# Linear attention into a gated mixture of four causal heads: identity and mask from GpSimd's selections, with another written-out order

## The chip, the cores and the metric

One core of a Trainium2 chip runs the whole computation. The metric is the device time of one execution in microseconds (us); the number to compare is the median of several executions. The engines are named as the profile names them: PE is TensorE (matmuls; PEld are its weight loads), DVE is VectorE, ACT is ScalarE, POOL is GpSimd, and SP only issues DMAs.

## The reference

Inputs are `q`, `k`, `v` of 8 batches x 8 heads x 576 positions x 64, a feature matrix `w_phi` of 64x128, a gate, and projections for four experts. All is float32.

```python
def phi(x):
    proj = np.einsum('bhsd,df->bhsf', x, w_phi)
    proj = proj - np.max(np.abs(proj), axis=-1, keepdims=True)
    return np.concatenate([np.exp(proj), np.exp(-proj)], axis=-1)
q_p, k_p = phi(q), phi(k)
kv = np.einsum('bhsf,bhsd->bhfd', k_p, v)
z = np.sum(k_p, axis=2)
num = np.einsum('bhsf,bhfd->bhsd', q_p, kv)
den = np.einsum('bhsf,bhf->bhs', q_p, z)[..., None] + 1e-06
x = (num / den)            # heads side by side: 8 x 576 x 512
...
logits = x @ w_gate        # four experts, the best two are kept
for e in range(4):
    q, k, v = x @ wq[e], x @ wk[e], x @ wv[e]
    scores = 0.125 * (q @ k.transpose(0, 2, 1))
    scores = np.where(causal, -1000000000.0, scores)
    scores = scores - scores.max(-1, keepdims=True)
    a = np.exp(scores)
    a /= a.sum(-1, keepdims=True) + 1e-09
    out += gate_e * (a @ v @ wo[e])
```

## The kernel before, in words

The first half (linear attention) goes over 32 pairs of heads, four pairs to a batch. For a pair, PE projects the keys (`stream_k`, `stream_tail`), DVE takes the largest absolute value of each row and subtracts it (`center`, L413 and L415), ACT makes the two exponentials (`ek`), and PE sums them against `v` (`stream_kv`). The queries are projected with features on the partitions (`stream_q`), ACT or DVE copies them out (`evac_u`), POOL finds the largest absolute value across the partitions (`reduce`, L535), DVE subtracts it (L545), ACT makes two exponentials, and PE multiplies with `kv` (`stream_n`). DVE and ACT divide (`normed`), DVE transposes 32x32 blocks, and the rows go through HBM and come back as `xb`, split into a high and a low part for PE (a cast on ACT or DVE, then a subtraction on DVE, L183). For the first five pairs the queries are taken in plain float32 (L514), later ones split (L518).

The second half (`stream_b`) goes over 8 batches and two groups of two experts. It projects queries, keys, values and the gate (L178), makes the scores (L678), adds the causal mask on DVE (`soft`, L706), finds the maximum on POOL (`first_top`'s selections at L693, then `tops` at L535), subtracts on DVE (L813), exponentiates on ACT, multiplies with the values (L427), normalises, and projects out (L178). The identity is read only at the end, where the last batch's result is transposed on PE (`turned`, L473). The mask is read from the first scores on.

All these streams are Python generators. `Plan.loop` takes their steps in the order of a table of characters, `PICKS`: of each two characters the first names the stream that takes its next step, the second the PSUM bank, or whether ACT or DVE does a copy that either could do. `in_order` then fixes that order on each engine, so every engine runs its own list strictly one after the other. The table also sets the order in which SP issues DMAs. One thing more is fixed by hand: DVE instructions with SBUF operands are noted in `plan.port`, and each of POOL's maxima waits for the one noted last (`plan.behind`), so that the two don't run at the same time.

`constants` (L225 to L236) makes the identity and the mask on DVE by fifteen small instructions: a row of column numbers by doubling, a transposed column of row numbers, and comparisons. It is called where the first batch's second half begins to be planned (L749), with two not yet used pieces of the scores' buffer as scratch.

Of the kernel before, what the change touches and what calls it, by code (L numbers as in the profile page):

```python
# [11 lines left out]
AF = mybir.ActivationFunctionType  # L12
# [45 lines left out]
    "DISASASASIF-UAUAVAVAOAUAQACAPAQATARATAOAJEPAFAFAKaJAKAJARADAPAMALAF-FIxANADAOAHAyAxAQAKsKANARAJHJAAAEBOAPAPAPAHARABAvAGA"
    "FAIAwAFAGAQAvATAUGQAQATHQASCLABAGAAALAtAOArAoAtAqAsAoAoAoAsAqApAOAMAnAVDqApAoAmAFsFIYaFIFAD-oAqApAqAoApAYIoArArAFsYaYIrA"
    "qApApAFstApApApItAqAqAqApAlADAlANADAD-SEoAnAqAlAnATFPDSCRAiAiAlAlABAAALAKAKAOGOBjAlAcAgANHEAjAKALAiAKAcAjACACAhAcAgAfAFA"  # L60
    "cAIaIAjAhAiADAcADAHFHAdIMAcAHAcAiAiAiAiIiALALAaAAAaAcAgAfAKALAfAfAFAbAHCeAaAfAcAEGIsIAHAEDgAeAgALABAeACALAYAKAKAaAZAZAfA"
# [941 lines left out]
```

## Time and profile before

| what | us |
|---|---|
| median of 3 runs | 531.89 (531.48 to 532.16) |
| the profiled execution's own time | 530.78 |
| its span | 529.0 |
| PE busy | 521.7 (99%) |
| DVE busy | 489.7 (93%) |
| ACT busy | 383.6 (73%) |
| POOL busy | 205.5 (39%) |

The span runs from the first to the last instruction of the profiled execution; the 1.78 us by which its own time is longer lie outside it. Busy times are unions over an engine's instructions, without the instructions that only wait or issue DMAs. A matmul's end is modelled, so a full PE is not PE at its peak. "Idle before <- X" tells whose instruction ended an engine's idle time. The granted clock of PE is at its higher level of 2.4 GHz all through (0.999 on average).

### The profile page before, as it was taken

The numbers are of one execution on the slowest core, as the hardware profiler recorded it, in microseconds if no ns is written. First come the engines' busy times: TensorE is split into PE (matmuls) and PEld (weight loads), VectorE is DVE, ScalarE is ACT, GpSimd is POOL, SyncE is SP. The second block draws the span as 40 slices with busy tenths as digits, with TensorE's granted clock in tenths as the row PEclk, the third lists the DMA queues.
The fourth block names the chain that finished last, engine by engine and source line by source line (L and its number), as shares of the span: only waits on it lengthen the run. The fifth ranks groups of instructions, "written<-read, shape, count | busy, mean of one in ns | idle before, by whom it ended". The sixth has DMA issues, their size and how long they took to land.

```text
span 529.0 us, 21993 instructions
## 1 busy us (share of the span) xinstructions
PE 521.7 (99%) x9422; PEld 503.8 (95%) x9422; DVE 489.7 (93%) x1020; ACT 383.6 (73%) x713; POOL 205.5 (39%) x112
## 2 busy tenths in 40 slices
PE   8999999999999999999999999999999999999997
PEld 6999999999999999999999999999999999999996
DVE  5999999999999999999999999989997999997984
ACT  4999879798697976975866687686686656565562
POOL 4755373063352457206270326332564060212430
PEclk9999999999999999999999999999999999999999
DMA  8888466534842546654455544476463324523213
GB/s 206 222 207 209 126 173 169 127 95 124 195 115 76 137 113 190 164 167 123 108 138 150 148 140 121 131 188 176 101 171 115 101 53 128 156 80 101 69 70 113
DMA packets 102674, 72.69 MB, mean 137 GB/s; under 512 B 57136, under 2 KB 84144, under 8 KB 102576
## 3 DMA queue, kind: packets, MB, share of 16 engines
q1 hardware_dynamic: 102272, 70.93, 50.5%
q8 instruction: 74, 1.21, 1.0%
q10 hardware_dynamic: 304, 0.34, 0.2%
q14 instruction: 24, 0.20, 0.1%
HBM read 46.15 MB, written 23.00 MB: 131 GB/s over the span
## 4 chain that ended last, share of the span: by engine, by line
PE 91%; ACT 7%; DVE 1%; issue 0%; DVEq 0%; ACTq 0%
PE ps_c L178 40%; PE ps_c L427 31%; PE ps_c L678 7%; PE ps_c L373 5%; PE ps_c L518 4%; PE ps_c L491 2%; ACT ek L189 2%; ACT u L187 1%; ACT u L189 1%; ACT mx L189 1%; PE ps_c L514 1%; ACT xb L187 0%; PE ps_c L473 0%; ACT xq L189 0%; ACT qk L187 0%
## 5 line engine op out<-in xcount | busy, mean ns | idle before, releaser
L535 POOL PARTITION_ALL_REDUCE mx<-u x32 | 126.6, 3970 | 125.7 <-DVE qsl L183 43.6
L178 PE MATMUL ps_c<-xb,qk 128*128 128x256 f32 (+1 forms) x768 | 108.6, 296 | 0.2 <-ACT u L187 0.2
L178 PEld LDWEIGHTS ps_c<-xb,qk 128*128 128x128 f32 x768 | 103.2, 188 | 1.9 <-ACT u L187 0.6
L189 ACT ACTIVATE ek<-ek 128x1152 f32<-128x1152 f32 x64 | 75.0, 1171 | 4.9 <-DVE ek L415 4.3
L427 PE MATMUL ps_c<-v_in,ek 128*64 128x65 f32 x2048 | 71.8, 222 | 0.8 <-issue 0.4
L427 PEld LDWEIGHTS ps_c<-v_in,ek 128*64 128x64 f32 x2048 | 67.0, 138 | 2.7 <-POOL mx L535 0.6
L535 POOL PARTITION_ALL_REDUCE tops<-top x15 | 55.5, 3701 | 33.7 <-DVE top L719 23.0
L813 DVE TENSOR_TENSOR st<-st,tops 128x1152 f32<-128x1152 f32 (+4 forms) x75 | 58.4, 810 | 0.9 <-POOL tops L535 0.9
L189 ACT ACTIVATE st<-st 128x1152 f32<-128x1152 f32 (+3 forms) x60 | 50.8, 870 | 10.8 <-DVE st L813 10.6
L187 ACT COPY u<-ps_c 128x320 f32<-128x320 f32 (+3 forms) x118 | 43.8, 416 | 19.5 <-PE ps_c L518 10.5
L187 ACT COPY st<-ps_c 128x512 f32<-128x512 f32 (+1 forms) x96 | 43.5, 505 | 19.2 <-PE ps_c L678 12.4
L178 PE MATMUL ps_c<-yh,wo 128*128 128x320 f32 (+1 forms) x256 | 52.8, 299 | 0.0
L178 PE MATMUL ps_c<-vg,xb 128*128 128x260 f32 x384 | 50.3, 285 | 0.0
L427 PE MATMUL ps_c<-vl,st 128*64 128x65 f32 x1500 | 49.4, 222 | 0.4 <-issue 0.4
L427 PEld LDWEIGHTS ps_c<-vl,st 128*64 128x64 f32 x1500 | 47.5, 138 | 1.1 <-issue 0.8
L413 DVE TENSOR_REDUCE pmax<-ps_c 128x8 f32<-128x1024 f32 (+1 forms) x64 | 47.3, 745 | 1.2 <-PE ps_c L427 0.6
L178 PEld LDWEIGHTS ps_c<-vg,xb 128*128 128x128 f32 x384 | 47.6, 189 | 0.8 <-DVE st L200 0.2
L415 DVE TENSOR_TENSOR ek<-ps_c,pmax 128x128 f32<-128x128 f32 (+1 forms) x64 | 47.2, 744 | 1.1
L545 DVE TENSOR_TENSOR u<-u,mx 128x1152 f32<-128x1152 f32 x32 | 43.5, 1361 | 0.1
L178 PEld LDWEIGHTS ps_c<-yh,wo 128*128 128x128 f32 x256 | 40.8, 188 | 0.9 <-issue 0.2
L189 ACT ACTIVATE u<-u 128x1152 f32<-128x1152 f32 (+3 forms) x36 | 40.7, 1139 | 0.2
L189 ACT ACTIVATE mx<-u 128x1152 f32<-128x1152 f32 x32 | 37.3, 1169 | 3.7 <-DVE u L545 3.6
(133 smaller groups left out, 1111.3 us busy)
## 6 DMA issues: line engine op xcount, KB each, us to landing
v_in<-in_v_dram SPq DMA_DIRECT2D x32, 320.0 KB, 4.2
xb<-xd SPq DMA_DIRECT2D x32, 288.0 KB, 3.3
q_in<-in_qt_dram SPq DMA_DIRECT2D x57, 144.0 KB, 3.0
out_dram<-ot SPq DMA_DIRECT2D x28, 288.0 KB, 2.6
k_in<-in_kt_dram SPq DMA_DIRECT2D x32, 160.0 KB, 3.2
xd<-xt SPq DMA_DIRECT2D x64, 80.0 KB, 2.7
xd<-xt SPq DMA_DIRECT2D x64, 64.0 KB, 2.4
yl<-yd SPq DMA_DIRECT2D x14, 288.0 KB, 3.1
```

The source lines that it names most:

```text
L178: nc.tensor.matmul(o, a, b, start=start, stop=stop, skip_group_check=True)
L187: nc.scalar.copy(o, i)
L189: nc.scalar.activation(o, i, func, **kw)
L373: nc.tensor.matmul(o, a, b, start=True, stop=True, skip_group_check=True)
L413: nc.vector.tensor_reduce(out=m, in_=src, axis=AX.X, op=ALU.max, apply_absolute_value=True)
L415: nc.vector.tensor_tensor(out=to, in0=src, in1=m.unsqueeze(len(m.shape)).to_broadcast([*m.shape, 128]), op=ALU.subtract)
L427: nc.tensor.matmul(o, a, b, start=start, stop=stop, skip_group_check=True)
L518: nc.tensor.matmul(pp_[:, h, 0:s1 - s0], wfs[r, w_], x_[r, s0:s1], start=m == 0, stop=m == 2, skip_group_check=True)
L535: nc.gpsimd.partition_all_reduce(o, i, 128, op)
L545: dve(2 * S, [uk], [mk], port=True).tensor_tensor(out=U, in0=U, in1=M, op=ALU.subtract)
L678: nc.tensor.matmul(pp_[0:n_, e, o:o + q1 - q0], kk2[k_][r, 128 * j:128 * j + n_], q2[q_][r, q0:q1], start=m == 0, stop=m == 2, skip_group_ ...
L813: dve(2 * n, [sj[j]], [*key, mk], port=True).tensor_tensor(out=a, in0=a, in1=tops[x][0:m, :, 128 * j:], op=ALU.subtract)
```

## The change

Two memsets on POOL set the identity and the mask's tile to zero before the other memsets. `constants` then has three affine selections on POOL: where row and column are equal the identity gets 1.0, and where the column is below the row the mask gets -1e9 (the third fills the 64 columns that stand ahead of the mask for blocks that start in the middle). They are issued once, behind POOL's first maximum, in `phi_q` of pair 0. The call in `stream_b` is gone. And `PICKS` is another table throughout; its first line stands here for all of it.

```diff
 PICKS = (
-    "BEBFBABBBCBEBCBEAABAEICACAHACAG-GaGsQAQAOIOINAFDQAQAQAPAG-GaPAGsOARAPAAANAPIHAHAEAEAPANABADABAE-NANANADAIAFAKBKAFCQARAQA"
+    "BABCBCBABFBGBEBBAABAEaCACAGIG-GsOAPAPAAIOIFGHAQAPACANAGIGsPANASAHABADABANAIAOAEAGaSAEAOIHAOAE-DAPAPIAAEAMAPAJEJAMAJAMAEB"
...
+    for t in (ident, mask3):
+        nc.gpsimd.memset(t, 0.0)
+
-    def constants(col, row):
-        nc.vector.memset(col[:, 0:1], 0.0)
-        for k in range(7):
-            n = 2 ** k
-            nc.vector.tensor_scalar(out=col[:, n:2 * n], in0=col[:, 0:n], scalar1=float(n), scalar2=None, op0=ALU.add)
-        nc.vector.transpose(row, col[:, 0:32])
-        for k in range(1, 4):
-            r_ = slice(32 * k, 32 * k + 32)
-            nc.vector.tensor_scalar(out=row[r_, 0:1], in0=row[r_, 0:1], scalar1=32.0 * k, scalar2=None, op0=ALU.add)
-        nc.vector.tensor_scalar(out=ident, in0=col, scalar1=row[:, 0:1], scalar2=None, op0=ALU.is_equal)
-        nc.vector.tensor_scalar(out=mask, in0=col, scalar1=row[:, 0:1], scalar2=-1.0e9, op0=ALU.is_lt, op1=ALU.mult)
-        nc.vector.tensor_copy(mask3[:, 0:64], mask[:, 0:64])
+    def constants():
+        for t, fill, op in ((ident, 1.0, ALU.not_equal), (mask, -1.0e9, ALU.is_ge), (mask3[:, 0:64], -1.0e9, ALU.is_ge)):
+            nc.gpsimd.affine_select(out=t, in_=t, compare_op=op, fill=fill, base=0, pattern=[[1, t.shape[1]]], channel_multiplier=-1)
...
         reduce(2 * S, M, U, [mk], us, bass_isa.ReduceOp.absmax)
+        if not p:
+            constants()
...
         yield Step('PE', (), None, all_x(b * NP))
-        if b == 0:
-            constants(st[0][1][:, 0, 0:128], st[0][1][:, 0, 128:160])
```

In the lists that follow, lines after the diff's first hunk are numbered four to six lower in the changed kernel (L529 is L535 of before, L541 is L545), and its buffers' numbers are two higher (`u_105` is the `u_103` of before; `ek` keeps its numbers).

On POOL, at the start: the end of its memsets, then the first maxima of the queries (`ISA`; one such row has no names). Before:

```order
L270 MEMSET yq_138 64x4x32
L274 MEMSET vl 128x20
L275 MEMSET vl 64x264
L535 ISA
L535 ISA mx_107<-u_103 128x1152
L535 ISA mx_108<-u_104 128x1152
L535 ISA mx_109<-u_105 128x1152
```

And in the changed kernel:

```order
L264 MEMSET yq_140 64x4x32
L268 MEMSET vl 128x20
L269 MEMSET vl 64x264
L529 ISA
L529 ISA mx_109<-u_105 128x1152
L230 AFFINE_SELECT ident<-ident 128x128
L230 AFFINE_SELECT mask<-mask 128x128
L230 AFFINE_SELECT mask<-mask 128x64
L529 ISA mx_110<-u_106 128x1152
L529 ISA mx_111<-u_107 128x1152
```

The three selections stand between the first and the second maximum; the two added memsets stand further up in the list.

On ACT, from the first exponential of the keys (`ek_62`, pair 0) to those of pair 2. Before:

```order
L187 CAST wfs<-wf 128x128
L187 CAST qk<-ot_159 128x576
L189 ACTIVATE ek_62<-ek_62 128x1152 x2
L187 COPY u_105<-ps_c 128x2x4x32
L189 ACTIVATE mx_107<-u_103 128x1152
L189 ACTIVATE u_103<-u_103 128x1152
L187 COPY kv_99<-ps_c 128x260
L187 COPY u_105<-ps_c 128x2x4x32
L189 ACTIVATE ek_63<-ek_63 128x1152 x2
L187 CAST vg<-ot_160 128x4x64 x2
L187 CAST vg<-ot_160 128x8
L189 ACTIVATE ek_62<-ek_62 128x1152
```

And in the changed kernel, from the second exponential of pair 0 on:

```order
L189 ACTIVATE ek_62<-ek_62 128x1152
L187 COPY u_106<-ps_c 128x2x4x32
L187 COPY u_107<-ps_c 128x2x5x32
L189 ACTIVATE mx_109<-u_105 128x1152
L187 COPY kv_101<-ps_c 128x260
L189 ACTIVATE u_105<-u_105 128x1152
L189 ACTIVATE ek_63<-ek_63 128x1152
L187 CAST vg<-ot_162 128x4x64 x2
L187 CAST vg<-ot_162 128x8
L189 ACTIVATE ek_63<-ek_63 128x1152
L189 ACTIVATE ek_62<-ek_62 128x1152 x2
```

The cast of `wfs` is gone from ACT's list (it is the first instruction behind DVE's memsets now), and the casts of `vg` (weights of values and gate) have moved in between the two exponentials of `ek_63`.

On DVE, from the last instructions of `constants` to the fourth pair's `xb`, which the first batch's projection needs last. Before:

```order
L234 TENSOR_SCALAR ident<-st_131 128x128
L235 TENSOR_SCALAR mask<-st_131 128x128
L236 COPY mask<-mask 128x64
L580 STREAM_TRANSPOSE xt_119<-xq_113 128x640
L183 TENSOR_TENSOR xb_124<-xb_124 128x576
L545 TENSOR_TENSOR u_106<-u_106,mx_110 128x1152
L183 TENSOR_TENSOR xb_125<-xb_125 128x576
L183 TENSOR_TENSOR xb_126<-xb_126 128x576
```

And in the changed kernel:

```order
L183 TENSOR_TENSOR xb_125<-xb_125 128x576
L200 CAST qk<-ot_161 128x320
L576 STREAM_TRANSPOSE xt_121<-xq_115 128x640
L183 TENSOR_TENSOR xb_126<-xb_126 128x576
L200 CAST vg<-ot_162 128x4x64 x2
L200 CAST vg<-ot_162 128x8
L541 TENSOR_TENSOR u_108<-u_108,mx_112 128x1152
L183 TENSOR_TENSOR xb_127<-xb_127 128x576
L183 TENSOR_TENSOR qk<-ot_161,qk 128x320
L200 CAST xb_128<-xb_128 128x576
L183 TENSOR_TENSOR xb_128<-xb_128 128x576
```

`constants` is gone from this list, and casts of `qk`, `vg` and `xb` that ACT did before stand in it.

## Rows read from the trace of the kernel before

**Rows 1.** The page's span and busy times of each engine.

```profile
span 529.0 us, 21993 instructions
...
PE 521.7 (99%) x9422; PEld 503.8 (95%) x9422; DVE 489.7 (93%) x1020; ACT 383.6 (73%) x713; POOL 205.5 (39%) x112
```

**Rows 2.** Busy time in four stretches: stretch, length, busy of PE, PEld, DVE, ACT, POOL (instructions), clock, DMA.

```profile
4.75:20.00 15.25, 14.63 (x275) 12.40 (x276) 12.43 (x21) 11.89 (x22) 10.25 (x3) 1.00 1.00 233
20.00:62.00 42.00, 41.85 (x1066) 38.70 (x1062) 40.73 (x82) 41.52 (x71) 21.25 (x6) 1.00 0.79 201
62.00:300.00 238.00, 237.34 (x4367) 230.87 (x4367) 229.72 (x471) 180.74 (x337) 97.08 (x43) 1.00 0.53 136
300.00:526.00 226.00, 225.21 (x3701) 219.31 (x3699) 205.03 (x440) 148.03 (x284) 74.77 (x38) 1.00 0.43 121
```

**Rows 3.** Waits of PE's weight loads, 20 to 62 us: total us, times, longest.

```profile
PEld ps_c L427 <- DVE ek L415: 0.3, 1, 0.3
PEld ps_c L427 <- ACT u L187: 0.3, 1, 0.3
PEld ps_c L518 <- DVE qsl L183: 0.3, 1, 0.3
PEld ps_c L427 <- ACT u L189: 0.2, 1, 0.2
...
PEld ps_c L518 <- DVE ek L415: 0.2, 1, 0.2
...
PEld ps_c L178 <- ACT u L187: 0.2, 1, 0.2
```

**Rows 4.** DVE's timeline around `constants`: start us, duration us, engine, line, operation.

```profile
56.29 0.06 DVE L226 MEMSET st<- 128x1 f32 x1
...
59.00 0.19 DVE L236 COPY mask<-mask 128x64 f32<-128x64 f32 x1
```

**Rows 5.** POOL's timeline: its last memset, and the first three maxima.

```profile
2.81 0.31 POOL L275 MEMSET vl<- 64x264 f32 x1
...
8.19 3.94 POOL L535 PARTITION_ALL_REDUCE mx<-u  x1 [5.07 <-ACT u L187]
13.69 7.87 POOL L535 PARTITION_ALL_REDUCE mx<-u  x2 [1.56 <-ACT ek L189]
```

**Rows 6.** POOL's selections at L693 (ns min/median/max), and a meeting on the timeline.

```profile
L693 POOL TENSOR_SCALAR_AFFINE_SELECT top<-st x15: 406/472/1015, 80.1 to 489.9; 128x256 f32<-128x256 f32 x15
...
L693 POOL TENSOR_SCALAR_AFFINE_SELECT u<-u x1: 1564/1564/1564, 498.1 to 498.1; 128x256 f32<-128x256 f32 x1
...
389.47 1.01 POOL L693 TENSOR_SCALAR_AFFINE_SELECT top<-st 128x256 f32<-128x256 f32 x1 [4.03 <-ACT st L187]
...
388.87 1.35 DVE L545 TENSOR_TENSOR u<-u,mx 128x1152 f32<-128x1152 f32 x1
```

**Rows 7.** DVE's timeline: the subtractions of the first and the third maximum.

```profile
12.16 1.36 DVE L545 TENSOR_TENSOR u<-u,mx 128x1152 f32<-128x1152 f32 x1
...
22.42 1.35 DVE L545 TENSOR_TENSOR u<-u,mx 128x1152 f32<-128x1152 f32 x1
```

**Rows 8.** What changes sides: groups by line (busy us, mean ns), and ACT's timeline.

```profile
L189 ACT ACTIVATE xq<-ps_c,rd 64x64 f32<-64x64 f32 x37 | 11.2, 307 | 9.5 <-DVE xq L458 6.3 <-PE ps_c L427 2.4
L187 ACT CAST xb<-xb 128x576 fp32r<-128x576 f32 x27 | 17.9, 675 | 0.7 <-DMA xb<-xd 0.7
L467 DVE TENSOR_SCALAR xq<-ps_c,rd 64x64 f32<-64x64 f32 x27 | 7.5, 277 | 0.2
...
18.80 0.80 ACT L187 CAST vg<-ot 128x256 fp32r<-128x256 f32 x3
```

**Rows 9.** Timeline of ACT and PE: the second pair's exponentials, and the half behind the second.

```profile
16.52 2.38 ACT L189 ACTIVATE ek<-ek 128x1152 f32<-128x1152 f32 x2
...
19.71 1.10 PE L427 MATMUL ps_c<-v_in,ek 128*64 128x65 f32 x32
```

**Rows 10.** PE's timeline: the start of the first projection.

```profile
61.79 0.99 PE L178 MATMUL ps_c<-xb,qk 128*128 128x320 f32 x5
```

More of the change, by code (lines that the diff above doesn't have):

```diff
@@ L58 @@
[L58 to L61, printed above, removed]
@@ new lines @@
+    "RAOAGAFADADAMAMAJACAAAFAMADaQAPABAKsKAOAJBJAQAPAJAPAPAPAFaF-NACAGACAOAAAHARARAPANADARADADIECKjKAUAQAQAAAFISAFARATARAJFJA"
+    "F-FISARAGANABAQAJAMASASASADADAQAOAOAGANADaK-EFJAJAKAUAPAVACAFIWAVAGACAOASASANAPAOAEBFAKsKARARAJATARARIPAMARAUATATARIFaSA"
+    "DADASIDIRAF-UAJEJAWAUAVAVANAOAKaKAVAPATATABAOAQAFAFAF-FIJIRAPAPAOAAAQIPAMAGIVADADAQANAHIRAOAWAVAUAOAGAJsJAIHKAIAEBOIOABA"
+    "FAIARAGATAFAWAXGWHTAQAQAQAwAOAAAMABANASAPARATCRAuARArAuAqAsAsArALApAOACAOANApAXEF1FIPAqAoAaaD-qAoAPAFIFAasoApApAFIrArArA"
@@ new lines @@
+    "rAoAPAaaFsaIpApAqApApApAqIrApApAqAqADADAD-WFVErAoAoAnAmAnALALAKATDTChApAOARARBjAkAQEPGCAjAdAiAiAEHeAhIMABAOAiALAMALAIaIA"
+    "kAdAdAdAKAhAdAjAfAiADANAMAiAiAiIfAHFHAgAMANADAhAdAHAhAeIHHIaIAMAiAgAgAAAKAAAfAeAGAeAaAFAbAbAbAEFFAKAeAgAgAcABAHAEEbAHIbA"
+    "bAbAN-MAcAMAeAdAdAMsbAbAbADaeAeAcAcAcAcAcAeAeIF-FIfAfACAAAdACAKAeAdAZAcAcALsL-DAFAcAYAcADADIJAiCiDgAgAcADA6AdAbA7AdAdAgA"
+    "gB6ADA7AcA5AcA3AcAFAcA3ABAAAZA2AaADaXAFsF-cAHBHAEA3A5AXA2AaAFAaAHAHHIs1AbA1AIAHAIaaAaAHA0AaA2A1A2A2A2AaAaA2A2IaAaAaA2AaA"
@@ new lines @@
+    "0AFAIAEB3AI-IA1AGA1AasaAaAaAaA3A3A0A5A3ADA0A0A0IDA2A2A1A1A2AyAYAZAFaFIKACACA3A4A3I3IBAXAyA1A1A1Aj-4AjajI1I1ADs6AWA4A4AAA"
+    "xAia1AeG6A1A1AzA2A3AuA2A1AXAfH4IGA1AGAYGdEcFyAxADAFAFA1AWAxAvAaAWAwA2ApApAaBtAtAXA0AZDuAxAvIpAuAuIrADAJAYCFsFIXAXA;A.A/A"
+    ".AXABAAAqAmA,AFAD-HBHAHAHEEFHAEAqAqAqAXAqAqA/A,A/AnAnA,AXAlACAIRIAoA+A+AqAHAmA,AFAkA+AoAoAp-BAlAnAIspAIAoA*A)ADAGAAAnAoA"
+    "oAoADA(AoAHA,A(A*A*A*A(A(A(A(I+A+A+A+AHAlA)I)A+IHA)IGAjAkAWjWRD-*A*A+A+AlA+AFsFIWa.A,A.AFAWsmB,A,A*A+AFA,A)A+A+AlAmADADA"
@@ new lines @@
+    "/A.AnG(A)A)A(A%A%AlA_A)A%AFsFa,I(AMHkA)I8ABAAA$AFACAjAKDFA$A#A%I!A#AFRFsD-%A&A$A9A9A$AGDEEGAHRHA-A-A-A-A-A-AGA)A(A(A9A9A"
+    "9A!A9AhA5ABAFA-A8j8A8A8AEA8A-A_A6A-A-A#AFAAA6ABATA5A9I!A9ADA!A!A!A!I9AH-HAlF_A9A_A9A-A-A!IpaFI%A-A-I_ADA#IDsF-JBKCiA3A3A"
+    "2A$I_I8AFA3A!AjG8A8A3AlaJA7A9ADA9AFA5A8IFsk-FI8I2Aka7A7A7A0A8A6AxACA9A6I6A6AxADADsGBGAEGGAgHzA7A5I9A6I9A6A4A5A-I-AwA6ANA"
+    "dBdHNFJAxAZABA4A2A2ADA4AFAxAzAAAsAuAvAyAbGZDIA0A1ADAzApAwACACAxAsAMAAAKE>AJCWBDsqApAGAGAxAtAFA<ArAvA;IwAlAlAHRHA:AqAuAGA"
@@ new lines @@
+    "sAsArA.AtArArArArA,AGAs-EDGAHs/ArAWA+A+AmAHA*AWA.A,ApA)AkAJAnAnAnAnAVAGIlA(AmIVAHIkA&ACAiAiAjABAlA)A$AHAED%ADADAGCGA%A(A"
+    "%A&A&A&A&AjA$A*A(A(AFsF-(A(A*A(A(AiAGAVIjADa*I)IV-&AFA&A(A(AFAFs+A+A*A)A)AVIVsAA_A(A(AhA(I)AF-.A(A,ADA)ADADajHkG%A%A%I%A"
+    "#A$A$A_AkA&AjBKE%A%A$A7AJFKHBAFA&A4AAAHaEFCA!A#A&A9A9A9A9A9A9A9A9A&A9A%A5A9A$AGHHA$AGAFA_A#A9s9A5A6AfACAeACABAEG7AJA5A6A"
+    "GA9ADADA8A6A_A8A8A-A7A9A7A7AFI-I-An-nanI-A-ID-_A_A8A8A8A8A8IFans!A-A7A9A_AjD9AhCiG1A6A6I6A6A7A5A2A5AiH1AwI2A8A0A4A4A4A9I"
@@ new lines @@
+    "4A0AeAMBfDJE2I3AcHMFwArA0A3ItAyA2IcAJAaGJCKEXDwIpApAoAAAoAqAnAwIuAwAvAuAuAlAHIHAyAsAsAwAwAsAtsGHGADAsAsAsAmAsAsAsAXAuAoA"
+    "sAsAsAvADAECrAvAvIXAXAuAGIuIqArAFApAmAJAjAsAqApAHIHAqAqAGGGAlAmAAAqAqAsAsAsAsAsAsIWaqAFAqAqImAGAsAsAWIFsuAuAIAW-FaWsoAjA"
+    "lA*AqAqA+A)A*A)ABAFACACAJADI)AjA*A*A*ApD.ApC.A+AAA%A%A&A&A*AnA*ApGJDJHnELF#AlA-A9ADAhA_IfA_A8AgAgA-A_AhA!IDA7ADI-A8A_AGC"
+    "GAH-HAgAGAEFEC!A8A-A7A7A9A7AHj7A8IHA9A7A7A7A8A_A!A8A-A8A!A7A7A7A7AFA-A!A-A9A9AgA9ADA_A_A_I9AFa#ADA!AeAhAJACAdAAABAD1Fj9A"
@@ L97 @@
+    "BDBAAABAAA"
 )
```

55 lines of the change are left out of this document (17 added, 38 removed).

## The prediction

> **What bounds the kernel now.** I read the page first: TensorE (PE) is busy for 521.7 of the 529.0 us span, VectorE (DVE) for 489.7, ScalarE (ACT) for 383.6 and GpSimd (POOL) for 205.5 [rows 1]. The table by stretches says where each is full [rows 2]. From 4.75 us, where the first matmul of the computation starts, to 20 us PE is busy 14.63 of 15.25 us and is still being fed its first data. From 20 to 62 us, until the first 128-row projection, three engines are full at once: PE 41.85, DVE 40.73 and ACT 41.52 of 42.00 us. From 62 to 526 us PE is busy 237.34 of 238 and 225.21 of 226 us, DVE follows at 229.72 and 205.03, and ACT has room. So after 62 us there is next to nothing to win: 0.66 us and 0.79 us of open PE time in 464 us.
>
> A matmul's end is modelled, so I checked that "busy" by the waits of PE's weight loads, which come just ahead of the matmuls. From 20 to 62 us six of them name DVE or ACT: 0.3 + 0.3 + 0.3 + 0.2 + 0.2 + 0.2 = 1.5 us, of which ACT has 0.7 (u L187 twice, u L189) and DVE 0.8 [rows 3]. That 1.5 us is what a better order can win in the ramp.
>
> **The change, part by part.**
>
> *Removed from DVE: the fifteen small instructions of `constants`.* They run one behind the other from 56.29 us (the memset, the first) to 59.00 + 0.19 = 59.19 us (the copy of the mask, the last) [rows 4]: 2.9 us of DVE's queue, 0.6% of its busy time, and inside the ramp, the one stretch where DVE is as full as PE.
>
> *Added to POOL, first: two memsets (identity 128x128, mask 128x192) ahead of the others.* The nearest row is the memset of 64x264, 0.31 us; I take 0.3 us each, so POOL's preamble ends near 3.7 instead of 3.1 us. The first maximum starts at 8.19 us after 5.07 us of idleness that ACT ends [rows 5]. Cost: nothing; the cover is those 5.07 us, of which 0.6 go.
>
> *Added to POOL, second: three selections behind the first maximum.* Before, POOL idles 1.56 us there, from 12.13 to 13.69 us [rows 5]. No row shows a 128x128 selection. The nearest, on 128x256, takes 0.41 to 0.47 us where nothing disturbs it [rows 6], so three take 0.6 us (half the elements, half the time) to 1.4 us. Both fit into 1.56 us. But DVE's subtraction of the first maximum, two SBUF operands, starts as soon as that maximum is there: 12.16 us, 1.36 us long [rows 7]. The trace shows what such a meeting does: the selection at 389.47 us took 1.01 us and ended at 390.48, 0.26 us behind the subtraction that ran from 388.87 to 390.22; another took 1.56 us [rows 6]. So I expect the first selection to end near 13.52 + 0.26 = 13.8 us, and the other two 0.4 to 0.9 us after it: the second maximum starts at 14.2 to 14.7 instead of 13.69 us, 0.5 to 1.0 us late. Who waits for it? The second and third maxima run back to back, 7.87 us, to 21.56 us, and DVE takes the third one up at 22.42 us [rows 5, 7]: 0.86 us to spare. I take 0.5 us late, and so no cost; the ends are 0 and +0.1 us, and the bad case is a rival below.
> The Trainium skill says in "SBUF — State Buffer", section "SBUF: two separate sides", that a VectorE instruction with two SBUF inputs and a GpSimd instruction that reads SBUF exclude each other for the whole of whichever began first. By that rule the trace agrees (1.01 and 1.56 us against 0.41 us), and the order of the two could also be the other one: then the subtraction would be late by one selection, 0.2 to 0.4 us.
>
> *The order: same work, other queues.* The PE list holds 5978 matmuls in both kernels, and 137 places in both where one kind of block follows another; its rows up to the first projection do the same blocks, only in two places swapped. So PE's own work is unchanged, and its part of the sum is 0. What changes is who copies. Up to the fourth pair's `xb` in the ramp the lists show that ACT gives away four quarters of normalised rows (307 ns each [rows 8], 1.2 us), one group of `vg` casts (0.80 us), one `xb` cast (0.68 us), one `kv` copy and the `wfs` cast (both narrower than the `xb` cast; I take 0.35 us each): some 3.4 us off ACT's 41.5 us. DVE takes them over at nearly the same lengths (277 ns a quarter [rows 8]; the casts and the copy I take at up to 0.5 us), about 2.6 to 3 us: just what `constants` left free. So DVE's queue in the ramp stays as long as it was, and ACT's becomes about 8% shorter.
>
> What is that worth? Bounds: 0, if PE's work alone sets the ramp's length, and -1.5 us, if each of the six named waits goes. I take ACT's three, 0.7 us, less 0.2 us, because some of such a wait stays wherever the tiling changes: **-0.5 us**. DVE's 0.8 us stay, as DVE is not relieved.
>
> *The first 20 us.* ACT's list loses the cast of `wfs` and one 256-column copy ahead of the first exponential, so that may begin 0.3 to 0.5 us earlier. But behind it ACT now does the `vg` casts between the two exponentials of `ek_63`, 0.80 us [rows 8]. Before, that pair of exponentials ran from 16.52 to 18.90 us, and PE began on the second one's half at 19.71 us [rows 9]. With 0.80 us of casts and 0.4 us of one more copy ahead, less the 0.4 us won, it ends at 19.7 us: just in time. Sum: 0, with ends -0.4 and +0.5 us.
>
> *After 62 us and the end.* Copies and casts change sides between ACT and DVE, in both directions, with PE's blocks nearly in the old order. As only 0.66 + 0.79 us are open, the ends are -0.5 us (a third of that) and about +1.5 us (five new waits as long as the ramp's longest, 0.3 us [rows 3]). I take 0. The tail has the same shape: ten transposes, then 48 output matmuls, then a copy and a store.
>
> **Sum.** 0 (POOL) + 0 (start) - 0.5 (ramp) + 0 (rest) = -0.5 us. The profiled execution took 530.78 us, 1.78 us of it outside the span, and lies 1.1 us under the median of the three runs, 531.89 us. Its 530.78 would become 530.3 us; the median, which is what is forecast, **531.4 us**. A difference under 0.2% (1.06 us) can't be told from none.
>
> **Rivals.**
>
> 1. *The freed time is worth more: faster, 529.9 us.* If the ramp is one knot of three engines, 3.4 us off ACT may undo all six waits, 1.5 us, and 0.5 us of the open PE time after it or before 20 us may go as well: -2.0 us. For it: PE, DVE and ACT are all full in the ramp [rows 2]. Against it: PE at 41.85 of 42.00 us leaves almost no room by itself. Chance 0.26.
>
> 2. *The selections hold the second maximum: slower.* Place: POOL behind the first maximum. If each of the three met a DVE instruction with two SBUF operands and took the longest time seen, 1.56 us, the second maximum would start at 12.13 + 4.7 = 16.8 us, 3.1 us late, and the third maximum's subtraction, with 0.86 us to spare, 2.3 us late: 534.2 us, if PE has nothing else ready. It decides from 0.86 us of delay on. For it: the meeting of the first selection with the subtraction is certain. Against it: DVE's next instructions, the absolute maxima and subtractions of the keys, read PSUM, not two SBUF operands, and half of the fifteen selections of the one form took 0.47 us or less [rows 6]. Chance 0.06.
> "Perfetto Trace Analysis" of the Trainium skill, section "Optimizing Scalar/DVE Operations", speaks against such a move too: since the two engines share a read port, taking work from one to the other might not help.
>
> 3. *The new order meets waits that the old one avoided: slower, 533.2 us.* PE, DVE and ACT wait in strict order; one copy that stands too late behind an exponential (1.17 us each) stops PE. Two such stops of 0.6 to 0.7 us give +1.3 us. The `vg` casts between the exponentials are one candidate, where I found no time to spare; the tail, where DVE now casts two `yh` parts that ACT cast before, is another. Against it: the old order, equally tight, has no wait above 0.3 us in the ramp [rows 3]. Chance 0.16.
>
> **How the numbers follow.** My forecast, PE's work unchanged and a few tenths won, has 0.52, with a range of its own from 530.6 to 532.6 us; it puts 0.05 on over 0.2% faster and nothing on slower. Rival 1 counts as faster (0.26), rivals 2 and 3 as slower (0.22). So faster 0.31, same 0.47, slower 0.22. The range reaches from 529.7 us, a little past rival 1, to 533.3 us, which takes in rival 3 and leaves rival 2 outside.
>
> **What would show it.** Right: the stretch from 56 to 59 us on DVE holds no `constants`; the first projection (61.79 us before [rows 10]) starts 0.3 to 0.8 us earlier, ACT's named waits of PE in the ramp shrink, the first selection takes over 1 us and the second maximum starts between 14.0 and 14.8 us, and the stage after 62 us has its old length to 0.7 us. Wrong: PE gaps of 0.5 us or more that name ACT or DVE after 62 us, a second maximum after 15 us, or a first projection that starts later than before.

## The result, and the profile after

The changed kernel takes 535.58 us (median of 20 runs, 532.97 to 538.54 us) against 531.94 us (20 runs, 530.83 to 533.70 us): ratio **1.0061, 95% interval 1.0045 to 1.0076**, slower by 3.2 us by this ratio, by 3.6 us by the two medians. Forecast were 531.4 us and a range that ended at 533.3 us. The profiled execution took 535.18 us. All ratios in this document leave out two executions of 1290 us, one each of the later kernels k1 and k3.

The page's span and busy times, which answer to [rows 1]:

```profile
span 533.4 us, 21968 instructions
...
PE 524.9 (98%) x9422; PEld 505.5 (95%) x9422; DVE 491.6 (92%) x1014; ACT 381.5 (72%) x704; POOL 208.5 (39%) x117
```

The table by stretches, as [rows 2]: stretch, length, busy us of PE, PEld, DVE, ACT, POOL (instructions), granted clock, DMA share, GB/s.

```profile
4.75:20.00 15.25, 14.70 (x261) 12.12 (x260) 12.25 (x21) 11.81 (x21) 11.83 (x6) 1.00 1.08 235
20.00:62.00 42.00, 41.80 (x1072) 38.85 (x1066) 40.88 (x75) 39.96 (x64) 21.96 (x6) 1.00 0.76 196
62.00:300.00 238.00, 234.89 (x4331) 227.75 (x4331) 226.72 (x469) 176.15 (x327) 94.52 (x40) 1.00 0.52 135
300.00:526.00 226.00, 225.96 (x3717) 219.71 (x3715) 209.27 (x441) 150.31 (x290) 77.58 (x40) 1.00 0.43 119
```

ACT is relieved in the ramp as the order said, from 41.52 to 39.96 us; DVE stays at 40.88 us. But from 62 to 300 us PE is busy 234.89 us where it had been 237.34: 2.45 us more stand open, with the same clock (1.00 in both). DVE and ACT are both less busy there than before, so neither of them became the bound. From 300 to 526 us it is the other way round, 225.96 us against 225.21.

What PE's weight loads waited for from 64 us on, first in the kernel before, then in the changed one (us in total, times, longest; "issue" is a wait for nothing that the profile shows):

```profile
PEld ps_c L427 <- issue: 1.5, 4, 0.6
PEld ps_c L678 <- issue: 0.5, 3, 0.2
PEld ps_c L178 <- ACT u L187: 0.5, 1, 0.5
```

```profile
PEld ps_c L421 <- issue: 2.8, 6, 1.3
PEld ps_c L178 <- issue: 1.0, 5, 0.3
PEld ps_c L178 <- DVE xb L183: 0.6, 1, 0.6
PEld ps_c L512 <- issue: 0.5, 2, 0.4
PEld ps_c L674 <- issue: 0.5, 3, 0.2
```

All rows named issue add up to 3.3 us before and 5.3 us after; all rows that name an engine to 2.4 and 2.7 us. The waits that grew have no engine's name. They stand at matmuls of 65 columns (L421; L427 before), one of them 1.3 us long:

```profile
233.96 0.38 PEld L421 LDWEIGHTS ps_c<-kv,u 128*64 128x64 f32 x10
235.62 0.78 PEld L421 LDWEIGHTS ps_c<-kv,u 128*64 128x64 f32 x24 [1.29 <-issue]
```

A block of 36 such loads is cut in two here: its data is there, and its first ten are done.

**What such a stop is.** The page's list of DMA queues has one that carries instructions:

```profile
q8 instruction: 74, 1.21, 1.0%
```

Counted in the trace, PE issues 18,980 instructions (18,985 before), 74 pages of 256, and this queue has 74 packets of 16 KB. With PE's instructions numbered from 0, one long stop after the other stands at number 193 within a page (449, 6593, 8897, 9153, 10177, 11201). I take that to be where one page's instructions end and the next page's begin; there are 74 such numbers, as many as packets. Not every wait named issue is such a stop: of the 5.3 us above 2.5 are, of the 3.3 us before 1.2, and the others, of up to 0.4 us here, stand at other numbers. While PE does 65-column matmuls, 256 instructions last only 3.75 to 3.95 us; in stretches with wide matmuls they last up to 10 us and more. With the narrow ones the next page's fetch begins 0.2 us or more behind the preceding boundary, its packet takes 0.9 to 1.8 us, and where PE stopped, it went on 1.3 to 1.6 us after the packet had landed (up to 1.8 us in other runs). Taking 3.85 us for the page, 1.0 for the packet and 1.45 for what follows it, I estimate that a fetch which begins by about 1.4 us costs nothing, and that each us beyond costs about a us of PE. At the stop above the boundary was at 230.52 us and the fetch began at 232.94. What the DMA engines did in these 2.42 us (no row of q8 is in this window), and then until PE went on:

```profile
DMA packets 281, 0.54 MB, mean 223 GB/s; under 512 B 50, under 2 KB 50, under 8 KB 281
...
q1 hardware_dynamic: 281, 0.54, 82.9%
```

```profile
q1 hardware_dynamic: 261, 0.34, 44.5%
q8 instruction: 1, 0.02, 2.8%
```

They were 83% busy with data, mostly packets of about 2 KB. The Trainium skill ("Runtime: NRT & Kernel Launch", section "Instruction fetch mechanics") says that instructions are refilled in blocks of 16 KiB, 256 of them, by a DMA queue that the sequencer drives itself while it works on the current block, and that crossing a block's end is "mostly hidden". The trace agrees on the block and the queue; it does not agree that crossing is hidden where the matmuls are narrow, with the 1.29 us above.

**POOL's part** went as forecast. Rows that answer to [rows 5]:

```profile
3.23 0.31 POOL L269 MEMSET vl<- 64x264 f32 x1
8.09 3.94 POOL L529 PARTITION_ALL_REDUCE mx<-u  x1 [4.55 <-ACT u L187]
11.92 0.36 POOL L230 TENSOR_SCALAR_AFFINE_SELECT ident<-ident 128x128 f32<-128x128 f32 x1
12.17 1.72 POOL L230 TENSOR_SCALAR_AFFINE_SELECT mask<-mask 128x128 f32<-128x128 f32 x2
13.96 7.86 POOL L529 PARTITION_ALL_REDUCE mx<-u  x2
```

The first selection ran ahead of DVE's subtraction of the first maximum, which starts at 12.35 us instead of 12.16, and the two selections of the mask met it. The second maximum starts 0.27 us later than before, and DVE takes up the third at 23.01 us (22.42 before, [rows 7]). The `vg` casts do lie between the exponentials of `ek_63` now, as I had feared (compare [rows 9]), and PE does not wait for the second one: its half begins at 20.13 us, right behind the block ahead of it.

```profile
17.55 0.80 ACT L187 CAST vg<-ot 128x256 fp32r<-128x256 f32 x3
18.25 3.41 ACT L189 ACTIVATE ek<-ek 128x1152 f32<-128x1152 f32 x3
```

```profile
19.91 0.39 PE L485 MATMUL ps_c<-v_in,ek 128*64 128x130 f32 x4
20.13 1.10 PE L421 MATMUL ps_c<-v_in,ek 128*64 128x65 f32 x32
```

**The ramp's end.** DVE has no `constants` from 56 to 59 us [rows 4], yet the first projection starts at 62.94 us instead of 61.79 [rows 10], and stops once for `xb`; just ahead of it, from 61.86 to 62.54 us and so across the end of that window, PE's loads wait 0.7 us for ACT's `u` (L187):

```profile
62.94 1.77 PE L178 MATMUL ps_c<-xb,qk 128*128 128x320 f32 x10
65.09 2.17 PE L178 MATMUL ps_c<-xb,qk 128*128 128x320 f32 x13 [0.38 <-DVE xb L183]
```

The waits from 20 to 62 us that name DVE or ACT, which answer to [rows 3], are 0.3 + 0.3 + 0.2 + 0.2 + 0.2 = 1.2 us. ACT's part is 1.0 us instead of 0.7; I had expected 0.2:

```profile
PEld ps_c L421 <- ACT u L189: 0.3, 1, 0.3
PEld ps_c L421 <- issue: 0.3, 1, 0.3
PEld ps_c L421 <- ACT ek L189: 0.3, 1, 0.3
PEld ps_c L421 <- ACT xq L189: 0.2, 1, 0.2
PEld ps_c L512 <- DVE xq L452: 0.2, 1, 0.2
...
PEld ps_c L367 <- ACT u L187: 0.2, 1, 0.2
```

### The profile page after: what moved, and what is told of

The parts are those of the page before. It is cut to its first block, busy times and chain, and to the rows that moved or that the text cites. A ratio compares the mean times of both kernels' runs of the same rounds, so it can differ in the third digit from the quotient of the medians.

```text
span 533.4 us, 21968 instructions
## 1 busy us (share of the span) xinstructions
PE 524.9 (98%) x9422; PEld 505.5 (95%) x9422; DVE 491.6 (92%) x1014; ACT 381.5 (72%) x704; POOL 208.5 (39%) x117
## 4 chain that ended last, share of the span: by engine, by line
PE 62%; DVE 11%; issue 2%; DMA 0%; ACT 0%; DVEq 0%
PE ps_c L178 30%; PE ps_c L421 19%; PE ps_c L674 6%; PE ps_c L367 3%; PE ps_c L512 3%; DVE st L807 1%; PE ps_c L485 1%; DVE xq L452 1%; DVE u L541 1%; DVE top L715 1%; DVE ek L409 1%; DVE pmax L407 1%; DVE xt L576 1%; DVE xb L183 1%; DVE qsl L183 1%
## 5 line engine op out<-in xcount | busy, mean ns | idle before, releaser
L529 POOL PARTITION_ALL_REDUCE mx<-u x32 | 126.4, 3963 | 155.4 <-DVE qsl L183 42.8
L178 PE MATMUL ps_c<-xb,qk 128*128 128x320 f32 (+1 forms) x768 | 109.3, 296 | 0.4 <-DVE xb L183 0.4
L421 PE MATMUL ps_c<-v_in,ek 128*64 128x65 f32 x2048 | 71.7, 222 | 0.5 <-DMA v_in<-in_v_dram 0.3
L421 PEld LDWEIGHTS ps_c<-v_in,ek 128*64 128x64 f32 x2048 | 67.3, 137 | 2.8 <-issue 0.9
L529 POOL PARTITION_ALL_REDUCE tops<-top x15 | 54.2, 3614 | 25.6 <-DVE top L715 25.1
L187 ACT COPY st<-ps_c 128x288 f32<-128x288 f32 (+1 forms) x98 | 44.0, 501 | 16.2 <-DVE ps_c L702 7.2
L187 ACT COPY u<-ps_c 128x320 f32<-128x320 f32 (+3 forms) x116 | 43.0, 418 | 16.0 <-PE ps_c L512 8.7
L421 PE MATMUL ps_c<-vl,st 128*64 128x65 f32 x1500 | 49.8, 222 | 0.2
L421 PEld LDWEIGHTS ps_c<-vl,st 128*64 128x64 f32 x1500 | 47.3, 138 | 1.1 <-issue 0.2
L409 DVE TENSOR_TENSOR ek<-ps_c,pmax 128x1024 f32<-128x1024 f32 (+1 forms) x64 | 47.4, 745 | 0.8
L541 DVE TENSOR_TENSOR u<-u,mx 128x1152 f32<-128x1152 f32 x32 | 44.9, 1409 | 0.1
L421 PE MATMUL ps_c<-kv,u 128*64 128x65 f32 x1152 | 39.9, 222 | 2.0 <-issue 1.8
```

Of the source, the lines that this page charges most:

```text
L178: nc.tensor.matmul(o, a, b, start=start, stop=stop, skip_group_check=True)
L187: nc.scalar.copy(o, i)
L409: nc.vector.tensor_tensor(out=to, in0=src, in1=m.unsqueeze(len(m.shape)).to_broadcast([*m.shape, 128]), op=ALU.subtract)
L421: nc.tensor.matmul(o, a, b, start=start, stop=stop, skip_group_check=True)
L529: nc.gpsimd.partition_all_reduce(o, i, 128, op)
L541: dve(2 * S, [uk], [mk], port=True).tensor_tensor(out=U, in0=U, in1=M, op=ALU.subtract)
```

## The experiments

Ten of the eighteen runs were chosen to say which part of the change costs and where, the others what PE waits for. "Issue" below is the sum of PE's rows named issue in its waits. The orders are tables of 2525 steps over the same steps, so a kernel can take one piece from either.

**1. The two parts of the change, each alone.**

```diff
 # e1: the changed kernel with the old table; e2: the kernel before with these lines the other way round
 PICKS = (
-    "BABCBCBABFBGBEBBAABAEaCACAGIG-Gs...
+    "BEBFBABBBCBEBCBEAABAEICACAHACAG-...
```

> The changed kernel's selections on GpSimd, with the searched order of the kernel before. Theory A (the new order makes the loss, the selections cost nothing): 531.4 to 532.3 us, ratio 0.999 to 1.001. Theory B (the selections on GpSimd hold the second maximum and make the loss): 534 to 536 us, ratio 1.004 to 1.008.

> The constants left on VectorE as before, with the new order. Theory A (the order makes the loss): 535 to 537.5 us, ratio 1.006 to 1.010, the loss of the changed kernel and up to 2 us more, since VectorE has its 2.9 us of constants back somewhere in the ramp. Theory B (the selections make it): 531.5 to 532.5 us.

Measured: e1 **1.001 (0.9991 to 1.003)**, e2 **1.0119 (1.0092 to 1.0146)**. Theory A holds. The selections on GpSimd cost nothing, and with the old order they also gain nothing. With the new order they are worth 0.58% (1.0119 less 1.0061), 3.1 us: in e2 DVE's fifteen instructions end just ahead of the fourth pair's cast of `xb`, and PE waits for that cast:

```profile
65.40 0.20 DVE L236 COPY mask<-mask 128x64 f32<-128x64 f32 x1
65.51 0.45 DVE L200 CAST xb<-xb 128x576 fp32r<-128x576 f32 x1
```

```profile
66.02 0.41 PE L178 MATMUL ps_c<-xb,qk 128*128 128x320 f32 x1 [1.55 <-DVE xb L200]
```

The new order is made for DVE without these instructions, but loses more than they are worth elsewhere.

**2. Ramp or rest.** At step 300 (62 us, just ahead of the first projection) both tables have done the same steps and hold the same banks, so they can be joined there.

```diff
-PICKS = (new)                  # h1
+PICKS = (new[:300], then the other steps as in old)
-PICKS = (new)                  # h2
+PICKS = (old[:300], then the other steps as in new)
```

> The changed kernel's code; the first 300 steps (up to about 62 us, just ahead of the first projection) in the new order, all later steps in the old order; no bank differs. Theory R (the ramp of the new order costs about 1.9 us, its rest the other 1.4): 1.002 to 1.0055 of before. Rival all-ramp: 1.006 or more. Rival all-rest: 0.999 to 1.001.

> The reverse: the first 300 steps in the old order, the rest in the new one. Theory R: 1.001 to 1.004 of before. Rival all-ramp: 0.999 to 1.001. Rival all-rest: 1.005 to 1.007.

Measured: h1 **1.001 (0.9997 to 1.0023)**, h2 **1.0065 (1.0039 to 1.009)**. Theory R falls: the ramp has no part in it. I had read 1.9 us out of the two first profiles: at equal work done the changed kernel was that far behind at 80 us. But in e1's profile, with the old order, the first projection starts at 64.13 us, later than in the changed kernel; one profile's ramp varies by more than what I compared. (s2, below, moved a DMA in that ramp and was for the same reason aimed at nothing.)

**3. Where in the rest.** The tables meet again at steps 627 (130 us) and 1274 (262 us), with no bank to rename.

```diff
-PICKS = (old)                  # pB; the code is the changed kernel's in all three
+PICKS = (old[:627], new's steps up to 1274, then as in old)
-PICKS = (old)                  # pC
+PICKS = (old[:1274], then as in new)
-PICKS = (new)                  # pD
+PICKS = (new[:627], old's steps up to 1274, then as in new)
```

> The changed kernel's code in the old order, steps 627 to 1274 (about 130 to 262 us) in the new one; no bank differs. Theory P (most of the loss is late instruction pages in the stretches of narrow matmuls at 150 to 166 and 220 to 238 us): 1.0035 to 1.006 of before, PE's waits named issue 5 us or more after 64 us. Rival E (spread evenly over 463 us): 1.001 to 1.0025.

> Old order up to step 1274, the new one behind it (262 us to the end). Theory P: 1.000 to 1.0025 of before (a wait of 0.4 us at 427 us and pages that are late elsewhere than in the old order). Rival E: 1.003 to 1.0045.

> The new order with the old order's steps 627 to 1274. Theory P: 1.000 to 1.003 of before. Rival E: 1.0035 to 1.0055.

> The changed kernel unchanged, beside the three above: 1.0045 to 1.0075 of before by either theory.

Measured beside each other: pB **1.0037 (1.0021 to 1.0052)**, pC **1.0022 (1.0007 to 1.0037)**, pD **1.002 (1.0001 to 1.0038)**, c0 **1.0063 (1.0042 to 1.0083)**. pB and pC add up to c0, and pD is c0 less pB within the intervals. So 132 us of the kernel carry 2.0 us of the 3.3, twice their even share of 0.9 us; the 264 us behind them carry 1.2 us. That is theory P's forecast in the times; pB's issue is 4.8 us after 64 us, a little under the 5 us that it named.

The waits of PE's loads from 130 to 266 us, in every profile that has one order or the other throughout that stretch (and its loads unchanged):

| order there | kernels | issue, us | naming an engine, us |
|---|---|---|---|
| old | before, e1, h1, pC, pD | 0.6, 1.1, 0.7, 1.1, 0.4 | 1.8, 2.5, 2.2, 3.0, 2.6 |
| new | changed, c0, e2, h2, s1, s2, pB | 3.0, 4.1, 3.0, 4.5, 3.6, 4.2, 2.4 | 0.4, 0.4, 0.6, 0.2, 0.2, 0.2, 0.4 |

In issue there is no overlap, 0.8 us against 3.5 us on average; of the difference 2.0 us stand at page ends. But the waits with a name fall by 2.1 us, so the sum of all waits rises by 0.7 us only and can't carry the 2.0 us by itself. Waits of weight loads pass in part under matmuls that still run, so I add the time itself. All these kernels have done the same matmuls when 2638 and when 5100 of the 9422 are issued (at some 130 and 262 us; s1 has 24 more ahead). From one to the other PE takes, in the order of kernels above (a stop is counted from the last start ahead of a page's end to the first start behind it, less the usual 0.055 us):

| order there | time, us | stops at page ends, us | mean time, stops, and time less stops |
|---|---|---|---|
| old | 131.99, 132.62, 132.12, 133.20, 132.38 | 0.1, 0.5, 0.4, 0.7, 0.1 | 132.46, 0.36, 132.10 |
| new | 133.92, 134.47, 133.93, 134.84, 132.87, 136.23, 133.33 | 2.2, 2.0, 1.8, 3.4, 1.4, 3.2, 1.4 | 134.23, 2.20, 132.03 |

The new order is 1.8 us longer in these profiles, its stops at page ends are 1.8 us longer, and without them the orders take 132.1 and 132.0 us on average (131.5 to 133.0 in single profiles). This is an account drawn from profiles: no run takes the stops away and leaves the order.

The rows of pB and of pD, which have changed places with each other in this stretch alone:

```profile
PEld ps_c L421 <- issue: 1.4, 3, 0.8
PEld ps_c L512 <- issue: 0.7, 2, 0.6
```

```profile
PEld ps_c L674 <- DVE u L200: 0.5, 1, 0.5
PEld ps_c L178 <- ACT u L187: 0.5, 1, 0.5
...
PEld ps_c L367 <- issue: 0.2, 1, 0.2
```

pD has the named waits, 0.5 us and less each. Outside that stretch issue is alike in both orders (2.3 to 3.2 us). What the new end costs is only partly found: at equal work done, the profiles of the changed kernel, c0, e2, h2, pC and pD fall 0.5 to 0.6 us further behind between some 410 and 460 us, and have there a wait of 0.3 us that the old end has not:

```profile
PEld ps_c L674 <- DVE yq L461: 0.3, 1, 0.3
```

The other half of its 1.2 us stays open.

**4. Is it the page?** If the stops belong to page ends, 48 more instructions ahead of everything move them to other matmuls.

```diff
-            for _ in range(3):
-                mm(t[1][:, 0:128], warm, warm, True, True, 128, t[0], [])
+            for _ in range(6):
+                mm(t[1][:, 0:64], warm, warm[:, 0:64], True, True, 64, t[0], [])
```

> The changed kernel with each warm-up matmul of 128 columns made as two of 64: 48 PE instructions more ahead of everything, the same order. Theory F (PE stops where an instruction page of 256 ends and the next one's fetch is late): the long gaps named issue after 62 us again stand at instruction 193 of a page, so at matmuls that lie 48 instructions earlier in the program, some vanish and others come; the time moves by up to 1.5 us either way, 534 to 537 us or 1.003 to 1.009 of before. Theory W (a hidden wait of those very matmuls): the gaps stay at the matmuls of the changed kernel (235.6 us 1.4 us long, 294.3 us 0.7 us) and the time within 0.5 us of it.

Measured: **1.005 (1.003 to 1.007)**. The long stops stand at instructions 5313 (1.31 us), 6337, 6593, 9153 (0.57), 10945, 14529, 15809 and 16065, all again number 193 of a page and so 48 instructions earlier in the program; beside the changed kernel's profile all of these but 6593 and 9153 are new, and those at 8897, 10177 and 11201 are gone. Which page ends show a stop is not fixed by this alone, since c0, the changed kernel once more, also has one at 5313 (0.82 us); the number within the page is. Theory F holds, and W, a hidden wait of certain matmuls, falls.

**5. Is it the loads?** Four trials, of different worth.

```diff
 # e3 (changed kernel), e4 (before): loads of k, q and v for p < 6 only
+            if p < 6:
                 load(v_ins[p % 2][:, :, 0:64], ...
```

> The changed kernel without the loads of k, q and v from pair 6 on (old data is used again; the output changes). Theory F (part of the loss is PE's instruction fetches, which come late when the loads fill the DMA engines): PE's gaps of 0.3 to 1.4 us named issue after 62 us, about 3 us together, are gone, and the time is 1.5 to 3.5 us below the changed kernel's 535.6: 532 to 534 us. Theory W (the loss is waits of the new order on other engines and the loads have no part in it): 535 to 536 us and the same gaps.

> The kernel before without the same loads. Theory F: its two gaps named issue at 286 and 354 us (0.67 and 0.64 us) are gone, 530.5 to 531.3 us, so that the distance to the run without loads of the changed kernel is 1.5 to 3 us, smaller than 3.6. Theory W: 531.5 to 532.2 us, and a distance of 3.2 to 4 us.

Measured: e3 **1.0017 (0.9996 to 1.0039)**, e4 **0.996 (0.9944 to 0.9977)**. Both gain about 2 us, but the distance between them, 3.8 us, is as large as before: in this the expectation of theory F failed. Stops remained: of 0.84 us in e3 and 1.03 us in e4 (at 231.8 and 161.4 us), while the DMAs of `xd`, `yd`, `yl` and `xb` still ran; the DMA engines were 81% and 43% busy while the two fetches were due. In the stretch from 130 to 266 us issue fell from 3.5 to 2.3 us with the new order and rose to 1.6 us with the old. The loads of k, q and v are thus not the whole traffic, and without them the two orders still differ by as much; their stops at page ends after 64 us, 1.0 us (e3) and 1.7 us (e4), do not make that difference, so something besides pages must. It lies elsewhere: from the 2638th to the 5100th matmul their profiles take 133.1 us (e3) and 133.2 us (e4), no longer 1.8 us apart, and from there to the last matmul 264.1 and 262.0 us. With one profile of each this is a hint that in that stretch the loads matter, and no more.

```diff
 # k3: on SP's queue alone, new order: pair 21's q ahead, pair 21's k back
+q_in<-in_qt x2  (behind the writes of yd)
 ... yl, v_in, yl, xb<-xd
-q_in<-in_qt x2, k_in<-in_kt x3
 xd<-xt
+k_in<-in_kt x3
```

> The new order, every engine's rows the same but two loads moved on SP's queue: pair 21's q (issued at 229.5 us) goes ahead to about 221, and pair 21's k (230.8 us) back behind the writes of pair 16's x, to about 237. Theory P with its cause (the loads hold up the fetch of PE's page that is due at 230.5 us): that fetch starts 1.0 to 1.8 us after its boundary instead of 2.2 to 3.4, the gap at instruction 9153 falls from 1.4 to 2.2 us to under 0.5, and the time is 0.8 to 1.6 us below the changed kernel: 1.0025 to 1.0045 of before. Rival (the late page has nothing to do with these loads): the gap stays over 1 us and the time at 1.0055 to 1.007.

Measured: 1.0079 (1.0051 to 1.0107). The effect shows at its place: the stop at 8897 is gone, the one at 9153 is 0.79 us, and its fetch began 2.09 us behind the boundary, which lies between the two expectations. PE's waits from 220 to 240 us, in the changed kernel, then in k3:

```profile
PEld ps_c L421 <- issue: 1.5, 2, 1.3
```

```profile
PEld ps_c L421 <- issue: 0.7, 1, 0.7
```

The time shows no gain: the interval covers the changed kernel's 1.0061 and excludes what theory P expected of it. Relief at one place did not arrive at the end.

```diff
 # k4: old order, v loaded twice
+            for _ in range(2 if p > 5 else 1):
                 load(v_ins[p % 2][:, :, 0:64], ...
```

> The changed kernel's code in the old order, with the load of v issued twice from pair 6 on (320 KB more per pair, the same data to the same place). Theory F (bytes that move during narrow matmuls hold up PE's instruction fetches): PE's waits named issue after 64 us grow from 3.1 to 3.7 us to 5 to 8, the time to 1.002 to 1.007 of before. Rival (traffic does not touch PE's instructions): issue stays under 4 us, 0.999 to 1.002.

Measured: 1.0821 (1.078 to 1.0861), 44 us, ten times what I expected. Issue grew to more than 10 us in L422's rows alone, but its three longest waits (2.5, 2.5 and 3.4 us) stand far from any page's end; the stops at page ends are 1.8 us after 64 us, as in the other kernels with the old order throughout (1.2 to 1.9 us). Most of the rest is waits for ACT of up to 5.5 us, and ACT in turn waits 18.6 us for late reloads of `xb`:

```profile
PEld ps_c L422 <- issue: 10.4, 7, 3.4
PEld ps_c L422 <- ACT ot L187: 5.6, 2, 5.1
PEld ps_c L513 <- ACT u L187: 5.5, 1, 5.5
```

So it says nothing on pages, and it shows that the profile's name issue alone does not make a wait a stop at a page's end.

What lies beside the fetch that is due at instruction 9153, in all profiles without a change to the loads and with the same numbering (the time is that from the boundary to the fetch's start; its packet takes 0.9 to 1.8 us):

| order at 226 to 236 us | fetch starts after, us | stop at 9153, us |
|---|---|---|
| old (before, e1, h1, pC, pD, k2) | 1.53, 2.05, 1.80, 1.52, 1.56, 2.02 | 0.18, 0.60, 0.41, 0.74, 0.16, 0.52 |
| new (changed, c0, e2, h2, s2, pB, k1) | 2.42, 1.75, 2.17, 3.02, 3.41, 2.30, 2.12 | 1.37, 0.82, 1.09, 1.91, 2.19, 0.86, 1.09 |

In all thirteen cases the DMA engines are some 80 to 120% busy, by the packets' times, while the fetch is due. With the old order the packets in that time measure some 340 to 960 bytes on average (`xd` and `yd` rows), with the new order 1600 to 2000 bytes (loads of v, q and k). Load on the DMA engines goes with late fetches, but does not decide alone. Of the fetches for pages under 5.5 us behind 64 us, in all runs but k4, x1 and x2, 66 of 216 began 1.5 us or more behind the boundary where the engines were at least 75% busy, and 6 of 148 where they were under 25% busy. One of those six, in k1, began 1.99 us behind its boundary (419.30 us), with this in between, and PE stopped:

```profile
DMA packets 1, 0.01 MB, mean 4 GB/s; under 512 B 0, under 2 KB 0, under 8 KB 0
```

```profile
423.69 0.13 PEld L421 LDWEIGHTS ps_c<-kv,u 128*64 128x64 f32 x1 [0.48 <-issue]
```

The same 540 narrow matmuls from 218 us on take 16.7 us before and 18.3 us after.

**6. The order of the DMAs alone.** SP's sequence exchanged between the orders from 130 to 262 us, every other engine's left.

```diff
-SP's DMAs of steps 627 to 1274 in the engines' own order
+SP's DMAs of steps 627 to 1274 in the other table's order      # x1: new engines, x2: old engines
```

> The changed kernel with its rows on PE, VectorE, ScalarE and GpSimd as they are; SP's DMAs of steps 627 to 1274 (130 to 262 us) in the old order's sequence (a few of its 75 steps excepted, which another engine needs sooner). Theory S (SP's order puts the loads under the narrow matmuls' page fetches and makes the loss of this stretch): 1.001 to 1.004 of before, as pD, issue waits of PE after 64 us 4.5 us or less. Rival O (the order of PE, VectorE and ScalarE makes it): 1.005 to 1.0075, issue waits as in the changed kernel, 5.3 to 7. Mixed orders can add waits of SP's queue; those would be named by their DMA in PE's, ScalarE's or VectorE's waits.

> The reverse: the changed kernel's code with all engines in the old order and SP's DMAs of steps 627 to 1274 in the new order's sequence. Theory S: 1.002 to 1.005, as pB, issue waits 4.5 us or more. Rival O: 0.999 to 1.0015, issue 3.1 to 3.7.

Measured: x1 **1.046 (1.0431 to 1.0489)**, x2 **1.0258 (1.0222 to 1.0294)**. Neither theory: a queue in another kernel's order makes its head wait for an engine that is not so far, and everything behind it is late. In x1:

```profile
PEld ps_c L421 <- ACT st L189: 8.0, 1, 8.0
PEld ps_c L421 <- ACT ot L187: 6.1, 2, 5.5
```

Inconclusive on the question; whether the order of SP's loads or the engines' own order makes the pages late stays open.

**7. Misses aimed at the wrong place.** s2 moved one reload ahead on SP's queue in the ramp.

```diff
+xb<-xd            (pair 1)
 ot<-in_wts
 v_in<-in_v
-xb<-xd            (pair 1)
```

> The changed kernel with one DMA moved on SP's queue: the reload of pair 1's x (at 48.01 us) ahead of a load of weights and a load of v instead of behind them; all other engines the same. Theory Q (the new ramp is late since that reload lands at 53.4, holds the writes of pair 3's x until 53.5 and its reload until 63.8): pair 3's writes start 0.8 to 1.6 us earlier, PE's gap of 0.7 us at 64.4 shrinks to under 0.3, and the time is 0.4 to 1.3 us below the changed kernel, 1.0035 to 1.0055 of before. Rival D (VectorE's own work paces the ramp): no change, 1.0055 to 1.007.

Measured: 1.0072 (1.0049 to 1.0096), as rival D. Pair 3's writes started at 55.1 us in its profile, not earlier than 53.5. The two other hybrids, with joints at steps 838 and 1280 (172 and 262 us) where banks had to be renamed:

> The changed kernel's code in the old order, but steps 838 to 1280 (about 172 to 262 us) in the new order; 11 blocks lie in other banks than in either order. Theory P (half of the loss is one place: PE's late instruction pages between 226 and 236 us): 1.002 to 1.0045 of before. Rival E (the loss is spread evenly over the 463 us behind the ramp, 0.7 us per 90): 1.0005 to 1.002.

> The reverse: the new order, with the old order's steps between 838 and 1280. Theory P: 1.002 to 1.0045 of before. Rival E: 1.0045 to 1.006.

Measured: k1 1.0082 (1.0056 to 1.0108), k2 1.0062 (1.0042 to 1.0082). Both have waits of their own at or behind the joints (k1 1.5 us for DVE's `ql` at 177.7 us, 0.7 us for ACT's `ot` at 276.8; k2 1.6 us for DVE's `kv` at 293 us), so their times say nothing on the stretch; their stops at 9153 stand in the table of part 5. That is why the joints of part 3 were sought where the tables hold the same banks. No version that does the whole work is faster than the kernel before; e4 is, without most of its loads.

## Why the prediction was wrong

- **POOL, 0: right.** The second maximum started at 13.96 us (I had 14.2 to 14.7), and the kernel with the selections and the old order takes 1.001. Rival 2 did not occur. The meeting came the other way round: the first selection, for which I gave over 1 us, took 0.36 us ahead of the subtraction, and the two of the mask, which met it, took 1.72 us together.
- **Ramp, -0.5 us: wrong in size, measured 0.** ACT was relieved, by 1.6 us of the 3.4 worked out, and DVE kept full. But h1 stands at 1.001, where e1, with the old ramp, stands at 1.001 too. That DVE's freed 2.9 us were spent again is what e2 shows from the other side: with `constants` still on DVE the same order is 3.1 us slower than without.
- **"After 62 us ... I take 0": this is the step that failed.** It measured +3.5 us (h2, 1.0065). Its upper end, +1.5 us, was built from named waits, "five new waits as long as the ramp's longest". Over all that lies behind 64 us the named waits stayed where they were (2.4 and 2.7 us), and from 130 to 262 us, where 2.0 of the 3.3 us lie, they even fell. I had shown that PE was open for only 0.66 and 0.79 us and concluded that there was nothing to win, and from "PE's own work is unchanged" that its part of the sum was 0. PE's matmuls are the same (9422 in both traces; my 5978 is in none of them), but in that stretch PE stops 1.8 us longer at the ends of its instruction pages, whose fetches begin later there with the new order. The sum had no term for this. The kernel before had the sign of it, 1.2 us of stops at page ends after 64 us, two of them over 0.6 us; my reading of the waits stopped at 62 us [rows 3].
- **Rival 3** had the direction and the wrong mechanism: neither the `vg` casts nor the tail's `yh` casts stop PE. That its direction came true is luck. Two of my three signs of being wrong showed, a first projection that starts later and gaps of 0.7 us (ACT's `u`) and 0.6 us (DVE's `xb`) beside it; but by h1 and h2 these cost nothing in the end, and the loss lay where I had set no sign.
- **Shown:** the loss is the new order's, behind step 300; 2.0 of 3.3 us lie between 130 and 262 us; PE's stops at page ends are longer there in every profile of that order, by 1.8 us on average, and the profiles' times differ by just that. **Argued, not shown by a run:** that taking the stops away would give the time back. **Open:** what in the order makes the fetches late, since leaving out loads, moving two of them and exchanging SP's order gave no clean answer; why the orders stay 3.8 us apart without those loads (not between 130 and 262 us, by one profile of each); and half of the 1.2 us behind 262 us.

## What to carry to other kernels

Where TensorE is bound and runs long stretches of narrow matmuls, read its waits named issue over the whole kernel, and count its instructions: in this case a page of 256 that lasts under 4 us left its successor's fetch some 1.4 us of room, and what it cost beyond that had no engine's name. Check where such a wait stands before laying it to the end of an instruction page: in k4 the longest waits named issue stood elsewhere. Judge an order by hybrids joined where both orders hold the same state, not by two profiles: here the two profiles pointed to the ramp, and the hybrids to the opposite end.

## What the runs showed of the hardware that was not expected

- TensorE can stop for its own instructions: 0.2 to 2.2 us at number 193 of a 256-instruction page, in stretches where a page lasts 3.75 to 3.95 us. Mostly the DMA engines are then over 75% busy with data, but a stop of 0.56 us (k1, 423.7 us) came with the engines all but idle. The kernel before has three such stops after 62 us (0.18, 0.67 and 0.64 us).
- Their length differs from run to run, as the tables show (0.82 and 1.37 us for the same program); the changed kernel's 20 times spread over 5.6 us, the kernel before's over 2.9 us.
